# Unit 14's means ahead of unit 15's values, x stores ahead of most early weights, a buffer of its own for unit 15's x

## Chip, cores and metric

One core of a Trainium2 chip. The metric is device time in microseconds of one execution of the whole kernel. Three runs of the kernel before took 682.92, 684.72 and 686.47 us; the median, 684.72 us, is the time before.

## What is computed

Local and downsampled attention of 8 batches x 8 heads x 576 positions x 64, then a mixture of experts (4 groups of 4) on its 4608 rows of 512. Cut to what matters:

```python
q_d, k_d, v_d = (mean over 4 neighbours of q, k, v)
out_up = repeat(softmax(q_d @ k_d.T / 8) @ v_d, 4)           # every row 4 times
scores = where(|i - j| < 4, q @ k.T / 8, -1e9)
x = out_up + softmax(scores) @ v                             # laid out as (4608, 512)
g = argmax(x @ w_group); e = argmax(x @ w_expert[g])         # router: one group, one expert
out = weight(g) * weight(e) * (relu(x @ w1[g, e]) @ w2[g, e])
```

## The kernel before

**Units.** The attention runs in 16 units: unit u is a pair of batches (u // 4) and a pair of heads (u % 4). Per unit, PE makes the local scores (`s_local`) and the downsampled ones (`s_down`); their exponentials are transposed (`turn_e`, `turn_pd`). `out_down` makes the downsampled output, `turn_down` transposes it; normed, it is "the unit's means" here. `down_store` (SP, three transfers) writes the means to a DRAM tile `odd`, and `load_down` (SP, one transfer) reads them back into the third rows of the unit's window tile `vw`, in a layout in which one product adds them to the local result. `load_windows` (SP, two transfers of 378 KB) puts the unit's values in the other rows of `vw`. `x_bank u i` (i = 0 to 2, L452, 24 products each) multiplies the transposed exponentials `pt` with `vw`; `x_bank_out` copies each bank to the tile `x` on ACT (A) or DVE (D). `store_x` writes the unit's x (576 KB) to the DRAM tile `xd`, on ACT's queue (A) or SP's (S). `turn_x` transposes it for the router (L467), `turn_x_out` copies that to `xT`, and `logits` (L497) multiplies it with the router's weights. After four units a quarter of the tokens has its logits, and `scores_out`, `scores_turn`, `choose`, `places`, `lists` and so on make token lists, on DVE above all.

**Buffers.** `of(n, u)` (L112) picks a unit's buffer. From unit 14 (`LATE_UNITS`) on all tiles of `kept`, x among them, have buffer 0 only, since the other ones lie in the pool `inp`, which the step `change` closes to make room for weights; windows are `vw[u % 2]`. So units 14 and 15 share one x. E, the exponentials of local scores, has two tiles, for even and odd units.

**Early expert.** While the last quarter is still on its way, one expert is begun with 256 of its tokens out of the first three quarters: `early_expert` loads its number into a register of SP (L1549), `gather` fetches the tokens' rows from `xd` (POOL, two indirect transfers, L914), and `weights_in c` (c = 0 to 3) loads a chunk of its weights, 512 KB of w1 and 512 KB of w2 (SP, L881), into one of two raw buffers (c % 2). `weights_split c n` takes each apart, the high part on ACT (L886), the low part on POOL or DVE (L887). `turn_in k` transposes the gathered tokens (L964) and takes them apart too. `hidden f` (f = 0 to 7, L979) needs w1 of chunk f // 2, `project f` (L1028) w2 of chunk f // 2. The last tokens of this expert come by `gather_late` and `turn_late`. Then 15 other experts follow in order of size (`begin`, `main`).

**Order.** The attention and the early expert are issued under a manual schedule: each engine does its instructions in the order in which the steps stand in the string `ORDER` (L1401 to L1512), which the loop at L1571 reads. SP, ACT and POOL also issue DMAs, and a DMA that has to wait holds all that stands behind it on the issuing engine. PE's results lie in a ring of four banks (`ps`) and one more that each fifth result takes (`px`, `bank`, L179).

Of the kernel before, what the change touches and what calls it, by code (L numbers as in the profile page):

```python
# [9 lines left out]
F32 = mybir.dt.float32  # L10
# [9 lines left out]
P = 128  # L20
B, H, S, D = 8, 8, 576, 64
SD = S // 4
G = 9
W = 38
WW = 42
# [11 lines left out]
NU = 4 * NB  # L37
# [24 lines left out]
class Attention:  # L62
# [9 lines left out]
    def __init__(self, tc, q, k, vm, vw, idf, xd, left, right, dram):  # L72
# [34 lines left out]
        self.E = [cp.tile([P, G, WW, 3], F32, name=f"E{i}") for i in range(2)]  # L107
# [4 lines left out]
    def of(self, n, u):  # L112

        t = self.kept[n]
        return t[u % len(t) if u < LATE_UNITS else 0]
# [584 lines left out]
class Experts:  # L700
# [175 lines left out]
    def weights_in(self, st, e, c):  # L876
        src1 = self.w1[st.get("r", 0) > 1][ds(e, 1)].rearrange("a (k p) f -> p (a k) f", p=P)[:, :, 256 * c : 256 * c + 256]
        src2 = self.w2[st.get("r", 0) in TURNED][ds(e, 1)].rearrange("a (k p) f -> p (a k) f", p=P)[:, 2 * c : 2 * c + 2, :]
        raw = self.raw[c % 2]
        for n, src in (("w1", src1), ("w2", src2)):  # L880
            self.nc.sync.dma_start(out=raw[n], in_=src)  # L881
# [616 lines left out]
load_windows 15; s_local_exp 15 1; turn_x_out 13 2 A; out_down 15; lists_places 2; turn_x 13 0; soft_down 15 P; turn_x 13 1; lists 2 P  # L1498
out_down_out 15 A; turn_down 15; turn_x_out 13 1 A; turn_down_out 15; turn_x_out 13 0 A; load_down 14 S; down_store 15 S; early_expert
lists_add 2; turn_e 14 2; logits 13; turn_e 14 1; early_list 1; turn_e_out 14 2 A; change; gather; turn_e 14 0; lists_out 2  # L1500
turn_e_out 14 1 A; turn_e_out 14 0 A; x_bank 14 2; x_bank 14 0; x_bank 14 1; x_bank_out 14 0 A; x_bank_out 14 1 A; turn_x 14 0
soft_local_sum 15 D; soft_local 15; x_bank_out 14 2 D; turn_e 15 0; store_x 14 A; turn_e_out 15 0 D; turn_x_out 14 0 D; turn_x 14 2
turn_x 14 1; turn_x_out 14 1 D; turn_x_out 14 2 A; weights_in 0; turn_e 15 1; turn_in 0; turn_e_out 15 1 D; weights_split 0 w1 P
load_down 15 S; logits 14; turn_in 1; weights_split 0 w2 P; weights_in 1; turn_e 15 2; turn_e_out 15 2 D; x_bank 15 0; turn_in 2
x_bank_out 15 0 A; x_bank 15 1; x_bank_out 15 1 A; x_bank 15 2; x_bank_out 15 2 D; turn_in 3; weights_in 2; turn_x 15 1; turn_x 15 2
turn_x_out 15 2 D; store_x 15 S; turn_x 15 0; weights_split 1 w1 P; turn_x_out 15 1 D; turn_x_out 15 0 A; hidden 0; weights_split 1 w2 P
weights_in 3; logits 15; scores_out 3; hidden 1; scores_turn 3; project 0; scores_turn_out 3; choose 3; choose_exp 3; choose_first 3
# [115 lines left out]
```

## Time and profile before

| | |
|---|---|
| median of 3 runs | 684.72 us (682.92 to 686.47) |
| the profiled execution's own time | 685.44 us |
| its span, first to last instruction | 683.7 us |
| mean granted clock of TensorE | 0.991 |
| PE busy | 642.7 us, 94% |
| PE's weight loads (PEld) | 573.8 us, 84% |
| DVE busy | 489.3 us, 72% |
| ACT busy | 384.5 us, 56% |
| POOL busy | 353.7 us, 52% |
| HBM read / written | 129.48 / 31.03 MB, 235 GB/s over the span |

PE multiplies and transposes, PEld loads its stationary operands beside that, DVE is the vector engine, ACT the scalar engine, POOL is GpSimd, SP only issues DMAs. SPq, ACTq and POOLq rows are an engine's issuing. In a timeline a row merges neighbouring instructions of one line: start, duration from the first one's start to the last one's end, engine, line, operation, output <- inputs, shape, count, and in brackets the engine's idle time ahead of it and what ended that. An instruction that waits for several things is put down to the last one by the profile. q1 is SP's DMA queue, q10 ACT's, q0 POOL's; all run on the same 16 DMA engines.

### The profile page before, as it was taken

What the parts mean: (1) busy time and instruction counts of PE and PEld (TensorE: products, weight loads), DVE (VectorE), ACT (ScalarE), POOL (GpSimd) and SP (SyncE); (2) the same over time, 40 slices, a digit from 0 to 9 for tenths busy, and PEclk for the clock granted to TensorE, in tenths of its full rate; (3) what the DMA queues carried; (4) which work ended last, traced back from release to release, by engine and by line L of the source; (5) the groups of instructions that cost most, each with busy time, mean ns of one, the idle gap of its engine ahead of it and who ended that gap; (6) DMA issues with size and microseconds to landing.
All of it is one profiled execution on the core that took longest, in us unless ns stands there. A gap on an engine that the chain in (4) does not pass through costs nothing. (4 is left out here: it accounts for less than half of the span.)

```text
span 683.7 us, 17694 instructions
## 1 busy us (share of the span) xinstructions
PE 642.7 (94%) x6743; PEld 573.8 (84%) x6743; DVE 489.3 (72%) x942; ACT 384.5 (56%) x833; POOL 353.7 (52%) x394
## 2 busy tenths in 40 slices
PE   7788997998987899999999999999999999999996
PEld 3565776676765788999899999999999999999995
DVE  5987988988896587644646667776776776777751
ACT  8776765775764536645544446456456456456531
POOL 7957556667542553403240446557547556455521
PEclk9999999999999999999999999999999999999999
DMA  8788899889778618959786778989999989999920
GB/s 305 207 253 264 270 295 269 272 230 263 238 207 263 201 29 265 319 166 247 222 218 203 206 217 235 250 264 280 234 271 277 253 250 273 270 271 268 284 70 27
DMA packets 128080, 160.77 MB, mean 235 GB/s; under 512 B 25445, under 2 KB 92783, under 8 KB 127968
## 3 DMA queue, kind: packets, MB, share of 16 engines
q1 hardware_dynamic: 102496, 129.99, 65.7%
q0 software_dynamic: 7952, 20.47, 10.1%
q10 hardware_dynamic: 17520, 8.85, 4.8%
q8 instruction: 66, 1.08, 0.7%
q14 instruction: 46, 0.38, 0.2%
HBM read 129.48 MB, written 31.03 MB: 235 GB/s over the span
## 5 line engine op out<-in xcount | busy, mean ns | idle before, releaser
L1072 POOL DMA_INDIRECT out_dram<-yt,qo x110 | 130.2, 1184 | 133.2 <-DVE qo L831 107.9
L983 ACT ACTIVATE hh<-ph 128x256 fp32r<-128x256 f32 (+13 forms) x128 | 53.3, 418 | 185.9 <-PE ph L979 184.0
L979 PE MATMUL ph<-xh,w1h 128*128 128x256 f32 (+13 forms) x512 | 153.8, 301 | 2.9 <-issue 2.8
L979 PE MATMUL ph<-xh,w1l 128*128 128x256 f32 (+13 forms) x512 | 153.0, 299 | 0.5 <-issue 0.5
L979 PE MATMUL ph<-xl,w1h 128*128 128x256 f32 (+13 forms) x512 | 153.1, 299 | 0.0
L984 DVE SCALAR_TENSOR_TENSOR hl<-ph,hh 128x256 fp32r<-128x256 f32 (+13 forms) x128 | 59.1, 464 | 86.4 <-ACT hh L983 86.0
L1030 PE MATMUL y<-hh,w2h 128*128 128x396 f32 (+11 forms) x384 | 115.9, 302 | 0.0
L1030 PE MATMUL y<-hh,w2l 128*128 128x396 f32 (+11 forms) x384 | 115.2, 300 | 0.5 <-issue 0.5
L1030 PE MATMUL y<-hl,w2h 128*128 128x396 f32 (+11 forms) x384 | 115.2, 300 | 0.0
L979 PEld LDWEIGHTS ph<-xh,w1h 128*128 128x128 f32 x512 | 96.6, 189 | 4.9 <-issue 4.0
L979 PEld LDWEIGHTS ph<-xl,w1h 128*128 128x128 f32 x512 | 96.7, 189 | 0.9
L979 PEld LDWEIGHTS ph<-xh,w1l 128*128 128x128 f32 x512 | 96.6, 189 | 0.1
L887 DVE TENSOR_TENSOR w2l<-raww,w2h 128x1024 fp32r<-128x1024 f32 x61 | 74.6, 1223 | 26.8 <-ACT w2h L886 24.8
L887 DVE TENSOR_TENSOR w1l<-raww,w1h 128x1024 fp32r<-128x1024 f32 x61 | 74.6, 1224 | 23.4 <-ACT w1h L886 22.6
L914 POOL DMA_INDIRECT xg<-xd,gi x47 | 53.2, 1132 | 54.9 <-ACT share L927 25.9
L1030 PEld LDWEIGHTS y<-hh,w2h 128*128 128x128 f32 x384 | 72.3, 188 | 1.3 <-ACT w2h L886 0.7
L1030 PEld LDWEIGHTS y<-hh,w2l 128*128 128x128 f32 x384 | 72.3, 188 | 0.7 <-issue 0.7
L1030 PEld LDWEIGHTS y<-hl,w2h 128*128 128x128 f32 x384 | 72.3, 188 | 0.0
L886 ACT ACTIVATE w1h<-raww 128x1024 fp32r<-128x1024 f32 x64 | 67.3, 1053 | 6.1 <-PE phr L995 2.7
L886 ACT ACTIVATE w2h<-raww 128x1024 fp32r<-128x1024 f32 x64 | 67.1, 1050 | 1.0 <-DMA raww<-in_moe_w_dram 1.0
L1072 POOL DMA_INDIRECT out_dram<-yo,oi x14 | 15.9, 1134 | 53.5 <-ACT yo L1063 20.6
L452 PE MATMUL b_x<-vw,pt 126*32 126x128 f32 x1152 | 38.0, 275 | 3.9 <-DMA vw<-odd 2.4
(247 smaller groups left out, 1268.3 us busy)
## 6 DMA issues: line engine op xcount, KB each, us to landing
raww<-in_w1q_dram SPq DMA_DIRECT2D x52, 512.0 KB
raww<-in_w2q_dram SPq DMA_DIRECT2D x44, 512.0 KB
raww<-in_moe_w_dram SPq DMA_DIRECT2D x32, 512.0 KB
vw<-in_vw_dram SPq DMA_DIRECT2D x32, 378.0 KB
kt<-in_k_dram SPq DMA_DIRECT2D x16, 576.0 KB
qT<-in_q_dram SPq DMA_DIRECT2D x16, 576.0 KB
xd<-x ACTq DMA_DIRECT2D x15, 576.0 KB
vs<-in_vm_dram SPq DMA_DIRECT2D x16, 512.0 KB
```

What stands on the lines that cost most here:

```text
L452: self.nc.tensor.matmul(pt[32 * j : 32 * j + 32, t], self.of("pt", u)[:ROWS, 32 * lin : 32 * lin + 32], self.windows(u)[:ROWS, :, lin], st ...
L886: self.nc.scalar.activation(hi, raw, AF.Copy)
L887: eng.tensor_tensor(out=lo, in0=raw, in1=hi.bitcast(F32), op=ALU.subtract)
L914: self.nc.gpsimd.indirect_dma_start(out=xg[:w], out_offset=None, in_=self.xd[0:rows], in_offset=bass.IndirectOffsetOnAxis(ap=st["gi"][:w, ...
L979: nc.tensor.matmul(ph, a[:, k, cs], st[b][:, k, 0:C], start=(n == 0), stop=(n == 11))
L983: nc.scalar.activation(hh, ph, AF.Relu)
L984: nc.vector.scalar_tensor_tensor(out=hl, in0=ph, scalar=0.0, in1=hh.bitcast(F32), op0=ALU.max, op1=ALU.subtract)
L1030: nc.tensor.matmul(y, a[:, f % 2, cs], b, start=(f == 0 and n == 0), stop=(f == 7 and n == 2))
L1072: i = self.nc.gpsimd.indirect_dma_start(out=out, out_offset=bass.IndirectOffsetOnAxis(ap=index, axis=0), in_=y, in_offset=None, bounds_che ...
```

## The change

Three things. In the constructor, E's first tile becomes a flat tile that is large enough for a unit's x, and unit 15 keeps its x there, when unit 14's exponentials, the last that the tile holds, have been transposed. `weights_in` can load w1 or w2 alone. And `ORDER` has new lines from 207 us or so on: `load_windows 15` stands behind `load_down 14` and `down_store 15`; `early_expert` stands ahead of these; `store_x 14` moves from ACT's queue to SP's and stands ahead of w2 of chunk 0 and of chunk 1, with only w1 of chunk 0 ahead of it; `store_x 15` stands ahead of chunk 2; `load_down 15` follows w1 of chunk 0; on PE, `turn_e 15 2` and `logits 14` stand ahead of `turn_in 0`, and unit 15's transposes go in the order of its banks; the splits of chunk 0's w2 and of chunk 1 stand somewhat later; two copies go from DVE to ACT. All lines of `ORDER` that change:

```diff
-        self.E = [cp.tile([P, G, WW, 3], F32, name=f"E{i}") for i in range(2)]
+        flat = [cp.tile([P, G * (P if i == 0 else 3 * WW)], F32, name=f"E{i}") for i in range(2)]
+        self.E = [x[:, 0 : G * 3 * WW].rearrange("p (g w e) -> p g w e", g=G, e=3) for x in flat]
+        self.last = flat[0].rearrange("p (g f) -> p g f", g=G)
...
     def of(self, n, u):
 
+        if n == "x" and u == NU - 1:
+            return self.last
         t = self.kept[n]
         return t[u % len(t) if u < LATE_UNITS else 0]
...
-    def weights_in(self, st, e, c):
+    def weights_in(self, st, e, c, only=None):
...
         for n, src in (("w1", src1), ("w2", src2)):
-            self.nc.sync.dma_start(out=raw[n], in_=src)
+            if only in (None, n):
+                self.nc.sync.dma_start(out=raw[n], in_=src)
...
-load_windows 15; s_local_exp 15 1; turn_x_out 13 2 A; out_down 15; lists_places 2; turn_x 13 0; soft_down 15 P; turn_x 13 1; lists 2 P
-out_down_out 15 A; turn_down 15; turn_x_out 13 1 A; turn_down_out 15; turn_x_out 13 0 A; load_down 14 S; down_store 15 S; early_expert
+early_expert; s_local_exp 15 1; turn_x_out 13 2 A; out_down 15; lists_places 2; turn_x 13 0; soft_down 15 P; turn_x 13 1; lists 2 P
+out_down_out 15 A; turn_down 15; turn_x_out 13 1 A; turn_down_out 15; turn_x_out 13 0 A; load_down 14 S; down_store 15 S; load_windows 15
 lists_add 2; turn_e 14 2; logits 13; turn_e 14 1; early_list 1; turn_e_out 14 2 A; change; gather; turn_e 14 0; lists_out 2
 turn_e_out 14 1 A; turn_e_out 14 0 A; x_bank 14 2; x_bank 14 0; x_bank 14 1; x_bank_out 14 0 A; x_bank_out 14 1 A; turn_x 14 0
-soft_local_sum 15 D; soft_local 15; x_bank_out 14 2 D; turn_e 15 0; store_x 14 A; turn_e_out 15 0 D; turn_x_out 14 0 D; turn_x 14 2
-turn_x 14 1; turn_x_out 14 1 D; turn_x_out 14 2 A; weights_in 0; turn_e 15 1; turn_in 0; turn_e_out 15 1 D; weights_split 0 w1 P
-load_down 15 S; logits 14; turn_in 1; weights_split 0 w2 P; weights_in 1; turn_e 15 2; turn_e_out 15 2 D; x_bank 15 0; turn_in 2
-x_bank_out 15 0 A; x_bank 15 1; x_bank_out 15 1 A; x_bank 15 2; x_bank_out 15 2 D; turn_in 3; weights_in 2; turn_x 15 1; turn_x 15 2
-turn_x_out 15 2 D; store_x 15 S; turn_x 15 0; weights_split 1 w1 P; turn_x_out 15 1 D; turn_x_out 15 0 A; hidden 0; weights_split 1 w2 P
-weights_in 3; logits 15; scores_out 3; hidden 1; scores_turn 3; project 0; scores_turn_out 3; choose 3; choose_exp 3; choose_first 3
+soft_local_sum 15 D; soft_local 15; x_bank_out 14 2 D; turn_e 15 0; weights_in 0 w1; turn_e_out 15 0 D; turn_x_out 14 0 A; turn_x 14 2
+turn_x 14 1; turn_x_out 14 1 D; turn_x_out 14 2 A; turn_e 15 1; turn_e_out 15 1 D; turn_e 15 2; turn_e_out 15 2 A; load_down 15 S; logits 14
+store_x 14 S; weights_split 0 w1 P; weights_in 0 w2; weights_in 1; turn_in 0; x_bank 15 0; turn_in 1; x_bank_out 15 0 A; x_bank 15 1; turn_in 2
+x_bank_out 15 1 A; x_bank 15 2; x_bank_out 15 2 D; turn_in 3; store_x 15 S; turn_x 15 0; turn_x_out 15 0 A; weights_split 0 w2 P; turn_x 15 1
+turn_x_out 15 1 D; turn_x 15 2; turn_x_out 15 2 D; hidden 0; weights_in 2; weights_split 1 w1 P; logits 15; scores_out 3; hidden 1; scores_turn 3
+weights_split 1 w2 P; weights_in 3; project 0; scores_turn_out 3; choose 3; choose_exp 3; choose_first 3
 weight 3; hidden 2; project 1; places 3; places_out 3; project 2; weights_split 2 w1 P; lists_places 3; lists 3 P; count 3
```

## Rows read from the trace of the kernel before

**Rows 1.** The page's busy times: busy us, share of the span, instructions.

```profile
PE 642.7 (94%) x6743; PEld 573.8 (84%) x6743; DVE 489.3 (72%) x942; ACT 384.5 (56%) x833; POOL 353.7 (52%) x394
```

**Rows 2.** Table of stretches: busy us (instructions) by engine, granted clock, DMA share, GB/s.

```profile
core 0: us, PE busy (x) PEld busy (x) DVE busy (x) ACT busy (x) POOL busy (x), PEclk, DMA share, GB/s
228.00:231.00 3.00, 3.00 (x16) 3.00 (x15) 1.41 (x3) 1.46 (x3) 1.96 (x1) 0.51 0.61 169
231.00:252.00 21.00, 20.70 (x157) 17.87 (x156) 16.72 (x44) 8.33 (x16) 12.19 (x6) 1.00 0.34 97
...
300.00:684.00 384.00, 374.29 (x2639) 364.35 (x2638) 250.41 (x424) 195.05 (x319) 180.72 (x155) 1.00 0.82 231
```

**Rows 3.** PE's timeline, 214 to 235 us.

```profile
214.79 2.17 PE L452 MATMUL b_x<-vw,pt 126*32 126x128 f32 x72 [2.35 <-DMA vw<-odd]
216.91 0.55 PE L467 MATMUL b_xt<-idf,x 128*128 128x128 f32 x3
...
218.27 0.49 PE L371 MATMUL b_e<-idf,E 128*126 128x128 f32 x3
219.84 0.30 PE L964 MATMUL xt<-idf,xg 128*128 128x128 f32 x1 [1.08 <-DVE xT L175]
220.97 0.33 PE L964 MATMUL xt<-idf,xg 128*128 128x128 f32 x1 [0.82 <-DMA xg<-xd,gi]
...
222.49 0.86 PE L452 MATMUL b_x<-vw,pt 126*32 126x128 f32 x24
...
227.71 2.18 PE L467 MATMUL b_xt<-idf,x 128*128 128x128 f32 x9 [2.17 <-ACT x L173]
229.54 0.56 PE L979 MATMUL ph<-xh,w1h 128*128 128x256 f32 x1
...
231.74 0.64 PE L497 MATMUL lg<-xT,wr 128*32 128x256 f32 x8
...
232.53 0.38 PE L979 MATMUL ph<-xh,w1h 128*128 128x256 f32 x1
...
234.05 0.38 PE L574 MATMUL lgt<-idf,lt 128*128 128x128 f32 x2
```

**Rows 4.** SP's timeline, 206 to 228 us: the DMAs that it issues.

```profile
206.18 0.89 SPq L440 DMA_DIRECT2D odd<-odn  x1
207.16 1.99 SPq L209 DMA_DIRECT2D vw<-in_vw_dram  x2
209.53 0.68 SPq L445 DMA_DIRECT2D vw<-odd  x1
...
211.29 0.46 SPq L440 DMA_DIRECT2D odd<-odn  x1
212.96 0.98 SPq L881 DMA_DIRECT2D raww<-in_moe_w_dram  x2
215.23 0.76 SPq L445 DMA_DIRECT2D vw<-odd  x1
216.22 11.65 SPq L881 DMA_DIRECT2D raww<-in_moe_w_dram  x4
```

**Rows 5.** ACT's timeline, 212 to 228 us.

```profile
212.15 0.87 ACT L173 ACTIVATE pt<-b_e 126x384 f32<-126x384 f32 x2 [0.39 <-PE b_e L371]
...
217.54 0.37 ACTq L462 DMA_DIRECT2D xd<-x  x1
...
226.78 0.87 ACT L173 ACTIVATE x<-b_x 128x384 f32<-128x384 f32 x2 [2.58 <-DMA xd<-x]
```

**Rows 6.** DMA queues (packets, MB, share) in 217.0-218.5, 218.5-221.5 and 221.5-225.0 us, one each.

```profile
q0 software_dynamic: 135, 0.50, 85.1%
...
q1 hardware_dynamic: 608, 0.80, 95.8%
...
q10 hardware_dynamic: 1111, 0.56, 57.7%
```

**Rows 7.** POOL's timeline, 214 to 226 us.

```profile
214.70 1.06 POOL L914 DMA_INDIRECT xg<-xd,gi  x1 [0.31 <-issue]
222.80 2.38 POOL L887 TENSOR_TENSOR w1l<-raww,w1h 128x1024 fp32r<-128x1024 f32 x1 [7.04 <-ACT w1h L886]
```

## Prediction

> **What bounds the kernel now.** I read the page's busy times first: PE is busy for 94% of the span [rows 1], so the question is where the rest lies. A table of stretches answers it: from 231 to 252 us PE is busy for 20.70 of 21 us, and from 300 us on for 374.29 of 384 [rows 2]. The whole second part is thus a full PE queue, and a microsecond taken from PE's line ahead of 231 us should come off the end, provided that the side chains (router, late gather, weights) move forward with it. The diff only touches 207 to 239 us. There I read PE's timeline for its gaps [rows 3] and then, for what ended each gap, the timelines of SP, ACT, DVE and POOL and the DMA queues.
>
> PE stands idle four times [rows 3]. From 212.43 to 214.79 unit 14's products wait for its means, which SP issued at 209.53 behind 0.77 MB of unit 15's values, issued from 207.16 [rows 4]. At 219.84 and 220.97 PE takes up the two tiles of the early gather after waits of 1.08 and 0.82 us; the first row names a DVE copy, the second the gather's DMA, and I count both as the gather, since the same four transposes wait. From 225.54 to 227.71 PE waits for unit 15's x, which ACT cannot copy out before 226.78, since store_x 14, issued at 217.54, still reads that buffer [rows 5]. Why nine microseconds: between 218.5 and 221.5 us its queue (q10) moves nothing while SP's q1 moves 0.80 MB; its packets go from 221.5 on [rows 6]. [...] Nine transposes then take 1.83 us (227.71 to 229.54), where twelve took 1.36 at the full clock (216.91 to 218.27, so about 1.0 for nine), and the first hidden block 2.2 (229.54 to 231.74) against 1.5 for the second (232.53 to 234.05) [rows 3]. This is some 1.5 us. Gaps and clock make 7.9 us.
>
> **The change, part by part.**
>
> *Unit 14's means first.* load_down 14 waits, as before, for down_store 14 to land, so it is still issued at 209.53 to 210.21, now with an empty queue ahead. early_expert's register load slips into SP's wait before that and costs nothing; ahead of the weights SP has no such load left. Bounds for the landing: from below at once, from above the 2.46 us that the last piece of down_store 14 needed from the end of its issue (207.07) until SP could go on at 209.53, with another store in its way: 212.7. I take 212.5, when PE arrives. The last ACT copy of pt 14 ends at 213.02 [rows 5], but the third bank goes first (0.7 us). Unit 14's products start at 212.6 in place of 214.79.
>
> *PE's line up to the gather.* Products 2.12 us (214.79 to 216.91), twelve transposes 1.36, two more groups of three 0.5 each (turn_e 15 1, and 15 2, which moves forward from behind the gather), logits 14, which also move forward, 0.6 as the later logits do: 4.9 us together, with the overlap of the last ones, so PE is through at 217.5, or 217.7 with a wait for the copies. The two copies that change engine (from DVE to ACT, about half a microsecond each [rows 5]) get no price: they end ahead of the gap at the gather, below, which covers them; without it ACT would hold logits 14 for as long.
>
> *What SP now sends, in order.* Three pieces of down_store 15 up to 211.75 as before; then load_windows 15 (two issues, 2 us, to 213.8); weights 0 w1 at about 214.1 (before 212.96); load_down 15 at 214.6 (before 215.23); store_x 14 when the copies of x 14 are done, about 215.6 (before 217.54, on ACT's queue, which loses 0.37 us); weights 0 w2 and both of chunk 1 at 216.3 to 217.6 (before 213.56 and 216.22); store_x 15 when x 15 is out; chunks 2 and 3 behind it. Queued behind the new wait in store_x 14 are only weights that PE needs after 226 us.
>
> *The gather.* POOL is through with issuing it at 215.76, as before [rows 7]; the change moves nothing that its list needs. The trace serves transfers in the order of issue, across queues: the gathers (q0) pass at 217.0 to 218.5, 0.50 MB [rows 6], behind weights issued at 212.96, and ahead of load_down 15 and chunk 1, issued at 215.23 and 216.22; store_x 14 passes last. [...] With the order of issue and 0.33 MB per us: values of unit 15 from 212.8 to 215.1, w1 of chunk 0 (0.52 MB) to 216.7, gathers to about 218.2, 0.3 us sooner than before. PE got the two tiles 1.3 and 2.5 us after the bulk had passed (219.84 and 220.97 against 218.5). Bounds for the second tile: 217.7 (no wait) and 220.97 (as before). I take 220.2, nearer to before: the bulk is only 0.3 us sooner, and the tail may be shorter or not. So the 2.2 us of the first part mostly turn into a wait at the gather: **a new gap of about 2.5 us from 217.7 on**.
>
> *Unit 15's means.* Before, PE could only use them at 222.49, 7.3 us after their issue, behind chunk 0's w2 and both gathers. Now they stand behind w1 alone and beside the gathers: about 0.4 us behind these, bounds 218 and 221.9 (the same 7.3 us). I take 220.4.
>
> *Own buffer for x 15.* Nothing stands between product and copy any more; the 2.17 us go. Late next is the third bank's copy, in the next sum. The three products of unit 15 and two blocks of the gather's transposes took 3.05 us (222.49 to 225.54), and a third block, which now stands among them, adds 0.3. So unit 15's transposes begin at 223.8, take 1.0 plus 0.4 for copies that they and hidden 0 wait for, hidden 0 starts at 225.2 and ends at 226.7 at the full clock; logits 15 add 0.8 (231.74 to 232.53), and hidden 1 starts at 227.5 against 232.53: **5.0 us sooner**.
>
> *What must keep up.* ACT and POOL split the weights, 2.38 us a piece on POOL [rows 7]. Chunk 0's w1 is split before the gather lands; its w2 on POOL from 225.7 to 228.1, needed by project 0 at 229.4; chunk 1's w1 then ends at 230.6, and hidden 2 needs it at 231.0: the tightest cover. If it goes, PE waits until POOL's next end, up to 1 us. The router's chain starts at logits 15 and moves with PE, and so does the late gather with its gap. Nothing else on the way is given a price.
>
> *Sum.* 684.72 - 5.0 = 679.7 us. The profiled execution took 685.44 us for a span of 683.7, 0.7 us above the median; taken from its own time the sum would be 680.4, and the 0.7 is the difference between runs.
>
> **The rivals.**
>
> *The clock falls in the new gap.* For it: the gap at the gather (2.5 us) is as long as the one ahead of the fall before (2.17). Against it: a gap of 2.36 us at 212.43 left the clock at full speed; it fell only after the other three. Price as measured, 1.5 us: 681.2. Chance 0.17.
>
> *The gather lands later still* (other queues' transfers in its way), at 221.2 in place of 220.2: 1 us less, 680.7. Chance 0.12.
>
> [...] Chance 0.08.
>
> *The change does less than it says.* Chunk 1's split on POOL is not ready and gives back up to 1 us, or unit 14's means still land after 213 us. The second costs nothing before 215, since the gather's wait swallows it. 680.7, chance 0.04.
>
> *Slower: the gathers starve behind SP's queue.* If another queue is served only when q1 is empty, as q10 seems to be, the gathers come after all that SP now sends without a pause from 212.8 on: 0.77 + 0.52 + 0.15 + 0.59 + 3 x 0.52 = 3.6 MB, 10.9 us at 0.33 MB per us, so 223.7, plus 1.5 of their own and 1.3 of tail: 226.5. Then 3.4 us of products and transposes, and 5.0 from the start of unit 15's transposes to hidden 1 with the cold clock (227.71 to 232.53 took 4.8), put hidden 1 at 234.9, 2.4 us behind: 687.1. It decides as soon as the second tile comes after about 224. Against it: before, the gathers went ahead of load_down 15 and of chunk 1, which were in q1 already. Chance 0.04. The forecast keeps 0.55.
>
> **How the numbers follow.** The likeliest case gives 679.7. Its bounds: with no wait at the gather and the means at 218, unit 15's products start near 218.2 at most, 2.2 us sooner (677.5); with late means and the cold clock together 3 us are lost (682.7). With half a microsecond for the median of a few runs (they spread from 682.92 to 686.47) the range is 676.9 to 683.0; it leaves out the starving case and parts of others. 0.5% is 3.4 us, about what a measurement here can tell from no change, so faster means below 681.3: nearly all of the forecast and of round robin, three quarters of the late gather, half of the cold clock: 0.80. Slower, above 688.1, is only the starving case at its worst or a disturbance: 0.03. The rest is 0.17.
>
> **What would show it.** In the changed kernel: unit 14's products start near 212.6, right behind the transposes; PE's longest gap in this part is ahead of the gather's first transposes and ended by the gather's DMA; no wait on store_x in ACT's or DVE's timeline; hidden 1 near 227.5; the granted clock at 1.00 from 220 to 231; the late gather some 5 us sooner. I am wrong if PE waits for weights in hidden 2 or project 0, if the clock falls, or if the gain ahead of hidden 1 is not found again at the end.

## The result, and the profile after

The changed kernel took 690.53 us (median of 14 runs, 685.74 to 693.03) beside 684.85 us (14 runs, 679.81 to 689.52) for the kernel before: a ratio of 1.0076, 95% interval 1.0047 to 1.0105. By the ratio it is slower by some 5.2 us, where 5.0 us less were forecast. The profiled execution took 692.06 us for a span of 690.4, at a mean granted clock of 0.978.

The page's busy times of the changed kernel, which answer to [rows 1]: PE is busy for 5.2 us more, with the same 6743 instructions.

```profile
PE 647.9 (94%) x6743; PEld 579.5 (84%) x6743; DVE 488.1 (71%) x940; ACT 384.9 (56%) x835; POOL 350.9 (51%) x394
```

The same instructions take longer, so part of the loss goes with the granted clock, 0.978 on the mean where the kernel before had 0.991. The table of stretches of the changed kernel (busy us and instructions by engine, granted clock, DMA share, GB/s) shows where:

```profile
219.00:227.00 8.00, 5.97 (x79) 3.73 (x79) 1.27 (x3) 2.97 (x6) 2.35 (x1) 0.57 0.86 278
227.00:240.00 13.00, 11.25 (x96) 9.34 (x92) 8.47 (x16) 7.65 (x15) 8.53 (x4) 1.00 0.69 207
240.00:247.00 7.00, 4.68 (x17) 4.20 (x18) 6.68 (x17) 0.00 (x0) 4.04 (x3) 0.52 0.10 13
```

The granted clock is at 0.57 and 0.52, for 8 and for 7 us; before it was as low in this part once, 0.51 for 3 us [rows 2]. In the second of these stretches DVE is busy nearly all the time (6.68 of 7 us), POOL more than half of it (4.04), and PE does 17 matmuls: PE waits for somebody.

To compare traces I count from one event that the change does not touch, the transposes of the third bank of E 14. Here is that row of the kernel before, and the late gather's first transposes, where all that follows starts (PE's timeline):

```profile
210.57 0.50 PE L371 MATMUL b_e<-idf,E 128*126 128x128 f32 x3
...
252.41 0.44 PE L964 MATMUL xt<-idf,xg 128*128 128x128 f32 x2 [0.71 <-DMA xg<-xd,gi]
```

PE's timeline of the changed kernel, to be read against [rows 3]:

```profile
208.73 0.50 PE L375 MATMUL b_e<-idf,E 128*126 128x128 f32 x3
...
211.47 2.17 PE L456 MATMUL b_x<-vw,pt 126*32 126x128 f32 x72 [0.88 <-DMA odd<-odn]
...
218.92 0.30 PE L969 MATMUL xt<-idf,xg 128*128 128x128 f32 x1 [2.51 <-issue]
221.24 0.47 PE L969 MATMUL xt<-idf,xg 128*128 128x128 f32 x1 [2.03 <-DMA xg<-xd,gi]
221.65 1.51 PE L456 MATMUL b_x<-vw,pt 126*32 126x128 f32 x24
...
227.23 1.15 PE L471 MATMUL b_xt<-idf,E 128*128 128x128 f32 x9
...
230.76 0.39 PE L984 MATMUL ph<-xh,w1h 128*128 128x256 f32 x1
...
238.31 0.22 PE L624 MATMUL pos<-oh,tri 128*128 128x144 bf16 x1 [0.95 <-DVE oh L611]
...
242.32 0.80 PE L1033 MATMUL y<-w2h,hl 128*128 128x512 f32 x1 [3.12 <-DVE hl L989]
...
256.68 0.44 PE L969 MATMUL xt<-idf,xg 128*128 128x128 f32 x2 [0.30 <-DMA xg<-xd,gi]
```

Counted from the common event:

| us from the transposes of E 14's third bank | before | after |
|---|---|---|
| unit 14's products | 4.22 | 2.74 |
| the gather's second tile | 10.40 | 12.51 |
| unit 15's products | 11.92 | 12.92 |
| unit 15's transposes | 17.14 | 18.50 |
| hidden 1 | 21.96 | 22.03 |
| late gather's first transposes | 41.84 | 47.95 |

Two things are to be seen. Up to hidden 1 the change gains nothing: unit 14's products come 1.5 us sooner and the 2.17 us ahead of unit 15's transposes are gone, but the gather, and the low clock behind it (0.57 from 219 to 227 us), take both back. And behind hidden 1, where not a step of PE has moved, 6.1 us are lost: hidden 1 to the late gather took 19.9 us before and 25.9 after. In that part stand two waits that the kernel before had not, 0.95 us for the one-hot table of the router's choice (`oh`) and 3.12 us for `hl`, the low part of hidden 2, both made by DVE.

DVE's timeline of the changed kernel has two steps there that are far too long for their size:

```profile
234.49 2.16 DVE L599 TENSOR_TENSOR t<-lg,mx 128x180 f32<-128x180 f32 x1
...
238.66 2.33 DVE L669 TENSOR_SCALAR two<-sums 128x9 f32<-128x9 f32 x1
...
241.85 0.42 DVE L989 SCALAR_TENSOR_TENSOR hl<-ph,hh 128x256 fp32r<-128x256 f32 x1
```

The same two steps in DVE's timeline of the kernel before, with the step in front of them and one that the comparison needs later:

```profile
235.02 0.34 DVE L594 TENSOR_REDUCE mx<-lg 128x45 f32<-128x180 f32 x1
235.40 0.45 DVE L595 TENSOR_TENSOR t<-lg,mx 128x180 f32<-128x180 f32 x1
...
237.87 0.17 DVE L665 TENSOR_SCALAR two<-sums 128x9 f32<-128x9 f32 x1
...
240.36 1.01 DVE L636 TENSOR_TENSOR ge<-pos,steps 128x45 f32<-128x45 f32 x1
```

What runs beside them is in POOL's timeline, first of the changed kernel, which answers to [rows 7] (in brackets POOL's idle time and what ended it):

```profile
229.33 2.40 POOL L892 TENSOR_TENSOR w2l<-raww,w2h 128x1024 fp32r<-128x1024 f32 x1 [5.79 <-ACT w2h L891]
231.68 2.41 POOL L892 TENSOR_TENSOR w1l<-raww,w1h 128x1024 fp32r<-128x1024 f32 x1
234.03 2.42 POOL L892 TENSOR_TENSOR w2l<-raww,w2h 128x1024 fp32r<-128x1024 f32 x1
238.59 2.37 POOL L892 TENSOR_TENSOR w1l<-raww,w1h 128x1024 fp32r<-128x1024 f32 x1 [2.14 <-ACT w1h L891]
```

then of the kernel before:

```profile
233.26 2.39 POOL L887 TENSOR_TENSOR w2l<-raww,w2h 128x1024 fp32r<-128x1024 f32 x1 [1.84 <-ACT w2h L886]
238.91 2.40 POOL L887 TENSOR_TENSOR w1l<-raww,w1h 128x1024 fp32r<-128x1024 f32 x1 [3.26 <-ACT w1h L886]
```

Both long steps start while a weight split of POOL is under way and end with it: 236.65 against POOL's 236.45, and 240.99 against 240.96. The kernel before has the same pattern, small: L595 starts 0.25 us ahead of POOL's end and takes 0.1 us longer than its twins, L636 ends at 241.37 against POOL's 241.31. The reduction L594 lies wholly beside a split and takes its 0.34 us, and `hl` at 234.66 us, of whose two inputs one (`ph`) stands in PSUM, takes its 0.42 beside the same split. So the theory is that **a DVE step that reads two tensors from SBUF, or a small TENSOR_SCALAR, is held until POOL's running split ends**. The change pushed three splits together, the last of them into the router's chain, since chunk 0's w2 now stands behind unit 15's copies on ACT (5.79 us of POOL's idle time, ended by ACT's high part). The second hold follows from the first: before, L665 was through 0.87 us ahead of the split of chunk 2's w1 (238.04 and 238.91), and now the held L599 has moved its like into that split. The traces of the two kernels agree with it for the steps with two SBUF inputs (L599 2.16 us, L636 1.01 in place of 0.21); for the TENSOR_SCALAR they have one case, L669. Why such a step is held they do not show. The rivals: the new order itself makes DVE late, or the weights come late.

### The profile page after: what moved, and what is told of

Its sections match the earlier page's. It is cut to its first block, busy times and chain, and to the rows that moved or that the text cites. A ratio compares the mean times of both kernels' runs of the same rounds, so it can differ in the third digit from the quotient of the medians.

```text
span 690.4 us, 17700 instructions
## 1 busy us (share of the span) xinstructions
PE 647.9 (94%) x6743; PEld 579.5 (84%) x6743; DVE 488.1 (71%) x940; ACT 384.9 (56%) x835; POOL 350.9 (51%) x394
## 3 DMA queue, kind: packets, MB, share of 16 engines
q8 instruction: 66, 1.08, 0.7%
## 5 line engine op out<-in xcount | busy, mean ns | idle before, releaser
L1077 POOL DMA_INDIRECT out_dram<-yt,qo x110 | 128.2, 1165 | 137.4 <-DVE qo L835 112.1
L456 PE MATMUL b_x<-vw,pt 126*32 126x128 f32 x1152 | 39.9, 283 | 2.1 <-DMA odd<-odn 0.9
```

Of the source, the lines that this page charges most:

```text
L456: self.nc.tensor.matmul(pt[32 * j : 32 * j + 32, t], self.of("pt", u)[:ROWS, 32 * lin : 32 * lin + 32], self.windows(u)[:ROWS, :, lin], st ...
L1077: i = self.nc.gpsimd.indirect_dma_start(out=out, out_offset=bass.IndirectOffsetOnAxis(ap=index, axis=0), in_=y, in_offset=None, bounds_che ...
```

## The experiments

Offsets are counted from the same event, in each run's own trace. A trace shows one execution, whose time can lie some 4 us from the run's median. The kernel before was run beside each group, and ratios are against it.

**Two splits on DVE.** Chunk 1's w2 and chunk 2's w1 are taken from POOL.

```diff
-weights_split 1 w2 P; weights_in 3; project 0; scores_turn_out 3; choose 3; choose_exp 3; choose_first 3
+weights_split 1 w2 D; weights_in 3; project 0; scores_turn_out 3; choose 3; choose_exp 3; choose_first 3
...
-... project 2; weights_split 2 w1 P; lists_places 3; lists 3 P; count 3
+... project 2; weights_split 2 w1 D; lists_places 3; lists 3 P; count 3
```

> The changed kernel with the low parts of chunk 1's w2 and chunk 2's w1 made on DVE in place of POOL. Theory (collision): two small DVE steps of the router, L599 (2.16 us) and L669 (2.33 us), are long only because a POOL split of 2.4 us runs at the same time; with these splits on DVE they take about 0.45 and 0.2 us, project 2 waits under 1 us for the low part of hidden 2 (3.12 before), the clock stays at 1.00 from 240 to 247 us, and the time is 684 to 687. Rival (late gather): the loss is the wait for the early gather and the cold clock from 220 on; the two DVE steps don't matter for the end, and the time stays at 689 to 692.

Measured: 691.11 us, ratio 1.0112 (1.0054 to 1.0169). L599 takes 0.35 us and L669 0.17, and the wait in project 2 falls from 3.12 to 1.00, so the held steps go with POOL's splits. But the late gather comes at 46.6, only 1.4 sooner: DVE itself now does 1.31 and 1.22 us of splits in the same chain, and its two large list products, which now start beside POOL's work, take 2.33 and 2.93 us (1.36 and 1.72 in the changed kernel), so that PE waits 2.19 us for the lists. The run moves the load; it settles nothing on the time.

**The collision made in the kernel before.** One split and the load behind it move back by some steps; nothing else of the change is there.

```diff
-turn_x_out 15 2 D; store_x 15 S; ... turn_x_out 15 0 A; hidden 0; weights_split 1 w2 P
-weights_in 3; logits 15; scores_out 3; hidden 1; scores_turn 3; project 0; scores_turn_out 3; choose 3; ...
+turn_x_out 15 2 D; store_x 15 S; ... turn_x_out 15 0 A; hidden 0
+logits 15; scores_out 3; hidden 1; scores_turn 3; project 0; scores_turn_out 3; weights_split 1 w2 P; weights_in 3; choose 3; ...
```

> The kernel before with one thing moved: the split of chunk 1's w2 (POOL) and the load of chunk 3 stand behind the router's scores, so that POOL works while DVE chooses. Theory (collision): one DVE step of choose or weight is stretched to 1 to 2.4 us, a wait of 1 to 4 us appears at places 3 or project 2, the time is 687 to 691. Rival (late gather): the gather is untouched, 684 to 686.

Measured: 687.9 us, ratio 1.0076 (1.0042 to 1.0110), as slow as the whole change. DVE's timeline of this run:

```profile
233.32 2.06 DVE L605 TENSOR_TENSOR o<-t,m2x 128x180 f32<-128x180 f32 x1
235.41 0.31 DVE L607 TENSOR_TENSOR oh<-o 128x144 bf16<-128x144 f32 x1
235.64 0.34 DVE L663 TENSOR_REDUCE sums<-ex 128x45 f32<-128x180 f32 x1
236.01 1.98 DVE L664 TENSOR_TENSOR tw<-sums,o 128x36 f32<-128x36 f32 x1
```

and POOL's, with PE's wait:

```profile
232.67 2.51 POOL L887 TENSOR_TENSOR w2l<-raww,w2h 128x1024 fp32r<-128x1024 f32 x1 [2.88 <-ACT w2h L886]
235.56 2.38 POOL L887 TENSOR_TENSOR w1l<-raww,w1h 128x1024 fp32r<-128x1024 f32 x1 [0.39 <-ACT w1h L886]
...
239.46 0.50 PE L1028 MATMUL y<-w2h,hl 128*128 128x512 f32 x1 [2.78 <-DVE hl L984]
```

Now L605 and L664 are the held ones: 2.06 and 1.98 us in place of 0.35 and 0.20, each ended by the end of a split (235.38 against 235.18, 237.99 against 237.94). The reduction between them runs beside a split at 0.34 us. Which of these steps is held goes with where the split falls; PE waits for no weights here. The late gather comes at 44.0, and hidden 1 to late gather takes 22.4 us. The 2.2 us at the late gather are less than the 5.2 us of the ratio: the traced execution, 683.5 us, was the fastest of twelve, and where the other 3 us lie is not shown.

**x 15 in its own buffer, alone.** The kernel before with the diff's lines for E, `last` and `of`, and no change of `ORDER`.

```diff
+        self.last = flat[0].rearrange("p (g f) -> p g f", g=G)
...
+        if n == "x" and u == NU - 1:
+            return self.last
```

> The kernel before with one part of the change alone, the buffer of its own for unit 15's x. The wait for store_x 14 (2.17 us) goes and the clock need not fall: hidden 1 about 3.5 us sooner. Theory (collision): POOL's splits keep their places in the order, so they may or may not meet the router's steps; 681 to 685. Rival (late gather is the whole loss): 680.5 to 681.5.

Measured: 684.8 us, ratio 1.0025 (0.9993 to 1.0057); no collision, late gather at 41.6. The wait for store_x is gone from PE's line, and yet hidden 1 comes at 21.7 against 21.96: in this run the gather's tiles came later (waits of 2.22 and 1.48 us in place of 1.08 and 0.82), and behind these waits the granted clock was 0.82 from 211 to 222 us and 0.84 from 222 to 231. So the 3.5 us that were expected did not come: the 2.17 us were not there to be had by themselves.

**store_x 14 back on ACT's queue.** The changed kernel with that one store in its old place.

```diff
-store_x 14 S; weights_split 0 w1 P; weights_in 0 w2; ...
+weights_split 0 w1 P; weights_in 0 w2; ...
...
-soft_local_sum 15 D; ... turn_e 15 0; weights_in 0 w1; ...
+soft_local_sum 15 D; ... turn_e 15 0; store_x 14 A; weights_in 0 w1; ...
```

> The changed kernel with store_x 14 back on ACT's queue in its old place. If what delays the early gather is that store_x 14 now shares SP's stream with it, the second tile comes about 2 us sooner (10.0 us from POOL's first issue to PE's use in the changed kernel, 7.9 in the one before). If it is w1 of chunk 0 and the values of unit 15 beside it, it stays at 9.5 to 10. Theory (collision): the time stays within 2 us of 690.5 either way, since the DVE steps still meet POOL's splits. Rival (late gather): 2 us less for 2 us of gather, 688.

Measured: 688.17 us, ratio 1.0061 (1.0025 to 1.0097). The gather's second tile comes at 12.98, no sooner than in the changed kernel (12.51): on SP's queue this store does not delay the gather more than on ACT's. L599 and L669 take 2.16 and 2.33 us as there. Hidden 1 comes at 24.0, since PE here also waits 1.30 us for unit 15's means, and the late gather at 50.2, later than in any other run; the time is no longer than the changed kernel's for it.

**The two splits left out.** The cleanest test of the collision, since DVE gets no work in exchange.

```diff
-... early_list 1; turn_e_out 14 2 A; change; gather; turn_e 14 0; lists_out 2
+... early_list 1; turn_e_out 14 2 A; change; gather; zero_low 1 w2; zero_low 2 w1; turn_e 14 0; lists_out 2
...
+    def zero_low(self, st, c, n):
+        st.setdefault("zero", []).append((n, c))
+        self.nc.gpsimd.memset(self.ws[c][n][1].bitcast(F32), 0.0)
...
         self.nc.scalar.activation(hi, raw, AF.Copy)
+        if (n, c) in st.get("zero", ()):
+            return
```

> The changed kernel without the low parts of chunk 1's w2 and of chunk 2's w1: POOL writes zeros there right behind the gather, while it is idle, and the two splits (2.4 us each on POOL) that run beside the router's steps are left out, so the output lacks these two low parts. If POOL's splits hold up DVE's steps on the router's path (collision), choose 3 on DVE (L599) falls from 2.16 to about 0.45 us and the weight step (L669) from 2.33 to about 0.2, the PE waits at places 3 (0.95) and project 2 (3.12) go, the clock does not fall a second time, and the late gather's first transposes come about 20 us behind hidden 1, as before the change, in place of 25.9. The time falls by 4 to 6 us against the changed kernel, to about 685. Rival (order of the steps alone, or the weights that arrive late): the two DVE steps keep over 1.5 us or the waits stay, and the late gather comes 25 us or more behind hidden 1.

Measured: 684.62 us, ratio 0.9974 (0.9952 to 0.9997), against 1.0076 for the changed kernel, which was not run beside it: the difference of the ratios is some 7 us. DVE's two steps in this run, and the late gather's first transposes on PE:

```profile
232.70 0.35 DVE L599 TENSOR_TENSOR t<-lg,mx 128x180 f32<-128x180 f32 x1
...
235.06 0.17 DVE L669 TENSOR_SCALAR two<-sums 128x9 f32<-128x9 f32 x1
...
248.73 0.44 PE L975 MATMUL xt<-idf,xg 128*128 128x128 f32 x2 [0.21 <-DMA xg<-xd,gi]
```

The wait at places is gone, that in project 2 is 0.21 us, the clock does not fall a second time here (granted 1.00 from 229 to 250 us), and hidden 1 to late gather takes 19.75 us (21.41 to 41.16). Everything that the change lost behind hidden 1 is back. Loads and high parts stand where they stood; that the low parts were late is excluded by DVE's rows, since these steps use no weights.

**Chunk 0's w1 behind store_x 14.** What makes the gather later.

```diff
-... turn_e 15 0; weights_in 0 w1; turn_e_out 15 0 D; ...
+... turn_e 15 0; turn_e_out 15 0 D; ...
...
-store_x 14 S; weights_split 0 w1 P; weights_in 0 w2; ...
+store_x 14 S; weights_in 0 w1; weights_split 0 w1 P; weights_in 0 w2; ...
```

> The changed kernel with the load of chunk 0's w1 behind store_x 14 on SP's queue, so that half a megabyte less is in flight when the early gather starts. If the queues share the DMA engines (round robin), what is in flight on SP's queue beside the gather sets its length: the second gather tile comes to PE about 1 us sooner than in the changed kernel (11.5 in place of 12.5 us behind the transposes of the third bank of E 14), hidden 1 about 0.5 to 1 us sooner, and everything behind it as before this edit: the same two DVE steps over 2 us, late gather 25 to 26 us behind hidden 1. If gathers wait for transfers in the order of issue, the same second tile moves by the whole of w1's passage, 1.5 us or more. If neither (the gather's own tail), it stays within 0.4 us. The time alone can hardly tell: 689 to 691.

Measured: 690.07 us, ratio 1.0095 (1.0053 to 1.0136). The second tile comes at 10.4 in place of 12.5, hidden 1 at 20.4 in place of 22.0, and the two held steps and both waits stay to the hundredth: front and back of the loss are independent. So w1 of chunk 0 costs the gather 2.1 us. By the expectation a step of 1.5 us or more speaks for the order of issue. The DMA queues show how the bytes passed. In 216 to 218 us of the changed kernel (packets, MB, share):

```profile
q1 hardware_dynamic: 293, 0.35, 57.4%
q0 software_dynamic: 54, 0.19, 38.4%
```

and in the kernel before, first in 214 to 217 us, where q1 stands alone, then in 217 to 218.5 us:

```profile
q1 hardware_dynamic: 784, 0.98, 101.8%
...
q0 software_dynamic: 135, 0.50, 85.1%
q1 hardware_dynamic: 56, 0.08, 15.1%
```

In the kernel before the two queues passed one after the other: up to 217 us not one packet of the gather passed, then 0.50 of its 0.54 MB in 1.5 us. In the changed kernel they passed side by side, SP's q1 with about twice the bytes of q0, and the gather was drawn out: q0 moves 0.13, 0.19 and 0.22 MB in the three pairs of microseconds from 214 to 220. With w1 out of the way it moves 0.36 and 0.17 MB from 212 to 216, the first at a share of 70% beside 27% of q1. What decides between the two ways no run here shows.

**Unit 15's products ahead of the gather's tiles.** From here on I look for a version that keeps the front's gain. PE does all of `x_bank 15` and `turn_x 15`, then `turn_in 0` to `turn_in 3`; weights of chunks 0 and 1 are issued ahead of both stores of x; chunk 1's w1 and chunk 2's w1 are split on DVE.

```diff
+... load_down 15 S; weights_in 0; weights_in 1; logits 14; x_bank 15 0; x_bank_out 15 0 A; x_bank 15 1; x_bank_out 15 1 A; x_bank 15 2; ...
+store_x 14 S; store_x 15 S; turn_x 15 0; ... turn_x 15 2; turn_x_out 15 2 D
+turn_in 0; turn_in 1; turn_in 2; turn_in 3; weights_split 0 w2 P; hidden 0; weights_in 2; weights_split 1 w1 D; logits 15; ...
```

> A version meant to beat both. From the changed kernel: the weights of chunks 0 and 1 are issued ahead of store_x 14 and store_x 15, unit 15's products and transposes on PE stand ahead of the early gather's four tiles, which cover the gather's passage, and the splits of chunk 1's w1 and of chunk 2's w1 go to DVE, placed so that no POOL split lies beside the router's choice or weights but that of chunk 1's w2. If the collision of POOL and DVE and the gap at the gather are what the change costs, hidden 1 starts 15 to 18 us behind the transposes of the third bank of E 14 (before 21.97, changed 22.03), the late gather's first transposes 35 to 39 us (before 41.84, changed 47.96), and the time is 678 to 681. Rival (the gather, now with more on SP's queue beside it, comes later than unit 15's work lasts; or the chunk 0 splits become late): hidden 1 at 19 to 22, late gather at 40 to 44, time 682 to 687.

Measured: 685.14 us, ratio 0.9991 (0.9965 to 1.0018). No wait is left at the gather, and hidden 1 comes at 19.1. But unit 15's means hold PE for 3.32 us, and the one POOL split that I had left beside the choice stretches L599 to 2.01 us: late gather at 41.4, as the rival had it.

**Splits early, nothing else.** The kernel with w1 behind store_x 14, the splits of chunk 0's w2 and of chunk 1 moved forward.

```diff
+weights_split 0 w2 P; x_bank_out 15 1 A; ... store_x 15 S; turn_x 15 0; turn_x_out 15 0 A; weights_split 1 w1 P; turn_x 15 1
+turn_x_out 15 1 D; turn_x 15 2; turn_x_out 15 2 D; weights_split 1 w2 P; hidden 0; weights_in 2; logits 15; ...
```

> The kernel of the run with w1 behind store_x 14, and the splits of chunk 0's w2 and of both of chunk 1 forward by some lines, so that POOL is through with them before the router's choice starts on DVE; nothing is left out and no split changes its engine. Collision theory: the two DVE steps (L599, L669) fall from 2.16 and 2.33 us to about 0.5 and 0.2, the waits at places 3 and project 2 (0.95 and 3.12) go, hidden 1 stays at 20 to 21 us behind the transposes of the third bank of E 14, and the late gather's first transposes come about 20 us behind hidden 1, at 40 to 41 (changed kernel 47.96, before 41.84). Time 683 to 685. Rival (the splits only move the collision to other DVE steps, or ACT's high parts now hold up unit 15's copies): hidden 1 at 21.5 or later, or the late gather over 43.

Measured: 687.98 us beside 685.8, ratio 1.0017 (0.9983 to 1.0051). The same work on the same engines, only sooner, and hidden 1 to late gather takes 20.1 us in place of 26.3. The row of POOL's last early split and the two DVE steps:

```profile
233.96 2.40 POOL L892 TENSOR_TENSOR w2l<-raww,w2h 128x1024 fp32r<-128x1024 f32 x1
...
235.92 0.64 DVE L599 TENSOR_TENSOR t<-lg,mx 128x180 f32<-128x180 f32 x1
...
238.57 0.17 DVE L669 TENSOR_SCALAR two<-sums 128x9 f32<-128x9 f32 x1
```

L599 ends at 236.56, POOL's split at 236.36: the tail of the same hold. Hidden 1, at 21.8, is later than in the run without this edit (20.4): PE waits 2.75 us ahead of unit 15's third products, where the run before had 1.35, as the rival had it.

**The same cure in the version with the products ahead**, all splits of chunks 0 and 1 on POOL and early.

```diff
+weights_in 1; logits 14; weights_split 0 w1 P; x_bank 15 0; x_bank_out 15 0 A; ...
+store_x 14 S; weights_split 0 w2 P; store_x 15 S; turn_x 15 0; ...
+weights_split 1 w1 P; turn_in 0; ... turn_in 3; weights_split 1 w2 P; hidden 0; weights_in 2; logits 15; ...
```

> The version with unit 15's products ahead of the gather's tiles, with the splits of chunks 0 and 1 all on POOL and ahead of the router's choice, and chunk 2's w1 on POOL as in the changed kernel. The choice step L599 falls from 2.01 to about 0.5 us, the waits at places 3 and project 2 (0.80 and 1.00) go, hidden 1 stays at about 19 us behind the transposes of the third bank of E 14, the late gather comes at 39 to 39.5 (41.4 in that version, 41.84 before). Time 681 to 683. Rival (POOL's splits stack up and the weights of chunk 1 come late to hidden 2, or POOL's split of chunk 2's w1 holds up the steps of places): late gather at 41 or later, time 685.

Measured: 684.5 us beside 685.8, ratio 0.9996 (0.9963 to 1.0030). The trace is nearly as expected (hidden 1 at 19.5, late gather at 39.6, 2.3 us sooner than before), the time, expected at 681 to 683, is not below the kernel before's. In its profiled run PE loses 4.1 us of busy time against the kernel before between 500 and 540 us, more than the gain. The row of 500 to 540 us from the table of stretches, of this run:

```profile
500.00:540.00 40.00, 34.61 (x267) 33.94 (x267) 26.73 (x52) 19.62 (x33) 21.64 (x20) 1.00 0.89 252
```

The kernel before is busy there for 38.75 us at a DMA share of 0.93. PE's gaps in that stretch stand at the first matmul of a late expert and are put down to "issue", so what PE waits for is not shown. From the common event to the end it took 473.9 us, the kernel before 473.1. In the 14 profiles of this study the stretch from the late gather to the end took 430.2 to 441.7 us. The longest, 437.6 to 441.7 us, are those of the run with two splits left out and of the last two runs below, beside which the kernel before, too, took 691.73 us.

**Unit 15's values earlier on SP's queue.** Three positions, all in the last version:

```diff
-... load_down 14 S; down_store 15 S; load_windows 15
+... load_down 14 S; load_windows 15; down_store 15 S
```

> The same, with unit 15's values issued by SP between load_down 14 and down_store 15, where SP waits for unit 15's heads anyway, so that unit 15's means do not stand behind 0.77 MB of values. If these values set when the means land, unit 15's products start at 8 to 8.7 us behind the transposes of the third bank of E 14 in place of 10.4, PE's gap ahead of them falls from 3.3 to about 1.3 us, the clock does not fall there, hidden 1 comes at 16.5 to 17.5 and the late gather at 37 to 38; time 679.5 to 681.5. Rival (the means need some 7.2 us from their issue whatever lies ahead of them, as in all kernels so far; or the gather now decides): products still at 10 or the gather's tiles wait by 1 us or more, hidden 1 at 19, time as without this edit.

Measured: ratio 1.0023 (0.9988 to 1.0058). The rival holds, and for a reason that neither had. The rows of SP from the last piece of down_store 15 on:

```profile
211.68 0.51 SPq L444 DMA_DIRECT2D odd<-odn  x1
216.99 0.72 SPq L449 DMA_DIRECT2D vw<-odd  x1
```

The store now stands behind the values, so load_down 15 can be issued only 4.8 us after its issue (at most 1.9 in the version without the edit, where the store's issue ended at 208.34 and SP, which issued the values meanwhile, went on at 210.25); the means then take 3.8 us to PE (products at 220.79) in place of 7.3. What the means gained behind the values, the store lost to them. Late gather at 41.8.

```diff
-... load_down 14 S; down_store 15 S; load_windows 15
+... load_down 14 S; down_store 15 S; load_down 15 S; load_windows 15
```

> The version with all splits early, with unit 15's values behind load_down 15 on SP's queue. If transfers of one queue pass one after the other, the means (issued at 210 us) no longer stand behind 0.77 MB of values; the means take 3.8 us from their issue, as where nothing lies ahead, and the values decide, some 2 us sooner than the means did: unit 15's products at 8 to 9 us behind the transposes of the third bank of E 14 in place of 10.4, PE's gap there 1 to 2 us in place of 3.4, hidden 1 at 17 to 18, late gather at 37.5 to 38.5; time 680 to 682.5 if the end follows. Rival (the values, issued 2 us later, land later than the means did): products at 10 or later, hidden 1 at 19 to 20, time as without this edit.

Measured: ratio 0.9999 (0.9969 to 1.0029). Now the values themselves are late: products at 12.9, released by the load of `vw`. Late gather at 41.7.

```diff
-early_expert; s_local_exp 15 1; ...
+load_windows 15; early_expert; s_local_exp 15 1; ...
...
-... load_down 14 S; down_store 15 S; load_windows 15
+... load_down 14 S; down_store 15 S
```

> The version with all splits early, with unit 15's values ahead of load_down 14, as in the kernel before. If one queue's transfers pass in order, unit 14's means come late again (products at 4.2 us behind the transposes of the third bank of E 14, a gap of 2.4 us), but unit 15's have no values ahead of them and are there when PE is through with unit 14, at 9.2 to 9.6; no further gap over 0.5 us ahead of hidden 0, no clock fall there; hidden 1 at 17 to 18, late gather at 37.5 to 38.5; time 680 to 682.5 if the end follows. Rival (the means of 15 still take 7 us from their issue, or the gather decides now): a second gap of 1.5 us or more, hidden 1 at 19 or later.

Measured: 689.79 us beside 691.73 for the kernel before in the same group, ratio 0.9968 (0.9938 to 0.9997): by an interval that ends just below 1 this version is faster than the kernel before, by about 2 us, where its late gather comes 3.8 us sooner; the changed kernel stands at 1.0076. PE's timeline:

```profile
213.79 2.56 PE L456 MATMUL b_x<-vw,pt 126*32 126x128 f32 x72 [1.82 <-DMA vw<-odd]
...
219.42 2.17 PE L456 MATMUL b_x<-vw,pt 126*32 126x128 f32 x72 [0.31 <-DMA raww<-in_moe_w_dram]
...
248.13 0.44 PE L969 MATMUL xt<-idf,xg 128*128 128x128 f32 x2 [0.79 <-DMA xg<-xd,gi]
```

Unit 14 waits 1.82 us for its means, unit 15 0.31; unit 14's 72 products take 2.56 us, unit 15's 2.17, as long as unit 14's in the kernel before [rows 3], at a granted clock of 1.00; and the late gather comes at 38.0 (210.11 to 248.13), 3.8 us sooner than before. It is this version that leaves out the first part of the change, unit 14's means ahead of unit 15's values.

The whole study in one table (late gather in us from the common event; the ratio is the time):

| kernel | hidden 1 | late gather | ratio to before |
|---|---|---|---|
| before | 21.96 | 41.84 | 1 |
| changed | 22.03 | 47.95 | 1.0076 |
| before, split late | 21.61 | 44.01 | 1.0076 |
| before, own buffer | 21.67 | 41.59 | 1.0025 |
| changed, two splits on DVE | 22.33 | 46.56 | 1.0112 |
| changed, store_x 14 on ACT | 24.03 | 50.16 | 1.0061 |
| changed, two splits left out | 21.41 | 41.16 | 0.9974 |
| changed, w1 behind store_x 14 | 20.41 | 46.70 | 1.0095 |
| the same, splits early | 21.79 | 41.87 | 1.0017 |
| products ahead of the gather | 19.09 | 41.40 | 0.9991 |
| the same, all splits early | 19.49 | 39.58 | 0.9996 |
| the same, values ahead of down_store 15 | 21.88 | 41.83 | 1.0023 |
| the same, values behind load_down 15 | 21.82 | 41.69 | 0.9999 |
| the same, values as before | 17.96 | 38.02 | 0.9968 |

The time goes with the late gather rather than with hidden 1: over the 13 rows below the first the ratio's correlation is 0.83 with the one and 0.53 with the other. It is no exact measure: the latest gather of all, 50.16, goes with a ratio of 1.0061.

## Why the prediction was wrong

**Unit 14's means.** Right in kind. The products started at 2.74 in the common count, against a predicted 2.03 (212.6 less 210.57), since the wait did not vanish: 0.88 us are left of 2.35.

**The gather.** This is the first step that failed: "the trace serves transfers in the order of issue, across queues". It describes the kernel before, where q0 came after q1, but it did not carry over. The sum let the gather's 0.50 MB pass in 1.5 us behind w1; in the changed kernel they took some 6 us beside q1, and without w1 the second tile came 2.1 us sooner. It came at 12.5, where 9.6 was predicted (220.2 less 210.57), with a rival at 10.6 (221.2). That is 2.9 us. Why the queues passed one after the other in one kernel and side by side in the other stays open. Round robin, which has 0.08 in the sum of chances, is a term that no run shows; what the runs showed is that q1 moved 0.35 MB and q0 0.19 in the same two microseconds (216 to 218 in the changed kernel), and that the gather's second tile then came 2.1 us later than in the kernel before.

**The clock rival.** It came true, with a price of 2.2 us in place of 1.5. The gap at the gather became 2.51 and 2.03 us, the clock fell behind it (granted 0.50 from 222 to 225 us), and the products of unit 15 took 1.51, 1.51 and 1.26 us in three parts where one took 0.86 before [rows 3]. From the second tile to hidden 1 the prediction had 7.3 us; it took 9.5. That is 2.2 us. With these two the gain ahead of hidden 1 was spent: the 5.0 us became -0.1.

**What must keep up.** This is the step that turned the sign. The prediction looked at POOL's splits as producers for PE, found chunk 1's w1 for hidden 2 to be "the tightest cover", and said of the router that its chain "starts at logits 15 and moves with PE". The weights were in time. But the splits, each 2.4 us long, now lay beside the router's steps on DVE, and two of these were held by 1.8 and 2.2 us (2.16 less 0.35, 2.33 less 0.17). PE's two new waits make 0.95 and 3.12 us; the late gather's own wait falls from 0.71 to 0.30; the rest, 2.4 us, is nearly all the clock, which granted 0.52 from 240 to 247 us: behind the long wait PE took 4.8 us, from 242.32 to 247.16, for the steps that took 2.6 before. Together 6.1 us. Leaving the two splits out gave all of this back, moving them forward gave it back too, and moving one of them back in the kernel before made a loss of 2.2 us at the late gather, and a ratio as large as that of the change. That the splits' place delays the late gather is shown, not argued; how many of the 5 us at the end come from it is known only by the ratios.

**The sum.** 2.9 + 2.2 + 6.1 = 11.2 us, against a late gather that came 6.1 us later in place of 5.0 sooner, 11.1 apart; 0.1 is what the rounding leaves. The ends of the prediction's range are off by 0.1 and 0.2 from its own terms: 677.5 and 682.7 with half a microsecond on either side make 677.0 to 683.2.

**x 15 in its own buffer.** The wait went, as said, but alone it moved hidden 1 by 0.3 us only: PE reached the gather's waits (2.22 and 1.48 us) and a low clock (0.82, then 0.84) all the same.

**The slower rival** named the gather and its price at 2.4 us, from a second tile at 224. On the scale of the kernel before the tile came at 223.1; the starvation did not happen, the queues passed side by side, and the loss behind hidden 1 came from a place that no rival named.

What stays open: why ACT's queue got nothing between 218.5 and 221.5 us in the kernel before (with store_x 14 on that queue in the changed kernel it moved 0.02 MB up to 218 us after the store's issue at 214.10, then went on with shares of 28 to 32% beside q1), and why the last part of the kernel takes from 430 to 442 us. The premise that a microsecond taken ahead of 231 us comes off the end is not borne out one for one: 2.3 us at the late gather gave nothing in the run with all splits early, and a loss of 2.2 us there went with one of 5.2 us in time.

## What to carry to other kernels

When an elementwise step on GpSimd is moved, write down which VectorE steps run beside it at the new place, above all a serial chain of small ones with two SBUF inputs: here three of 0.20 to 0.35 us (L599, L605, L664) took 2.16, 2.06 and 1.98 us, to the end of the GpSimd instruction, a split of 2.4 us. In the changed kernel two holds cost 4 us of waits and 2.4 us of clock. Count what other queues have in flight when a gather starts: here 0.52 MB of weights on SP's queue cost the gather's second tile 2.1 us (12.51 in place of 10.41). And follow a gain past the edited stretch to the next point where all chains meet, here the late gather, before it is called a gain.

## What the hardware showed that was not expected

A 128x9 step of 0.17 us took 2.33 beside a GpSimd instruction, while reductions (0.34) and steps with an input from PSUM (`hl`, 0.42 at 234.66 us in the kernel before) ran beside one at their usual length. The hold goes to VectorE's large steps too: the 128x1152 and 128x576 products of the lists took 2.33 and 2.93 us with two splits on DVE, where the changed kernel had 1.36 and 1.72. And it goes both ways. The 1.72 us are themselves a hold behind POOL's share of the lists (L685), for the same step on DVE took 0.76 us at 207.40, while POOL stood idle. POOL's share took 1.16 us at 204.71, started ahead of DVE's large product, and 2.32 at 243.92, started behind it; the split that POOL started at 246.20 beside DVE's product took 2.92 us in place of 2.4.

A load that waits for a store to land was not helped by moving the values about near the pair: 0.77 MB of values cost some 3 us ahead of the store (4.8 us until SP could go on, in place of 1.9 at most) or between the two (7.3 us to PE in place of 3.8), and behind both they were themselves the last to come. What helped was to issue them ahead of unit 14's load as well, although PE then waited 1.82 us for unit 14's means.
